# One FFT and mixture-of-experts kernel: inputs laid out in the order of its first step, the multiplier table loaded whole, and one order of steps for all eight batches

## The chip, the cores and the metric

The kernel runs on one core of one Trainium2 chip. The time is the device time of one execution in microseconds (us). Three runs of the kernel before took 1506.66, 1509.06 and 1509.7 us; the median is 1509.06 us. Work that numpy does on the host before the launch is in no time.

The core's engines are TensorE (PE in the profile, with its weight loads as PEld), VectorE (DVE), ScalarE (ACT), GpSimd (POOL) and SyncE (SP). Sixteen DMA engines move data between the chip's memory and the on-chip buffers; transfers are issued by SP, ACT and POOL, each in the order of its own queue.

## What is computed

The input x is 8 batches of 2496 rows of 256 values. Each column of each batch is filtered in the frequency domain, and the result goes through a mixture of 8 experts with a capacity of 2496 rows each:

```python
X = np.fft.rfft(x, axis=1)                      # 8 x 2496 x 256 -> 8 x 1249 x 256
Y = X * (filt_r + 1j * filt_i)[None]
y = np.fft.irfft(Y, n=2496, axis=1).reshape(19968, 256)
logits = y @ w_gate                             # 8 logits a row
# rows go to experts in the order of falling logits, at most 2496 to each expert
out[mask_e] = np.maximum(y[mask_e] @ w1[e], 0) @ w2[e]
```

## The kernel before

The program has three parts, one after the other on TensorE. Until about 404 us the batches go through the transform (class `Fft`); until 479.5 us the last step of the inverse transform runs together with the search for the experts' thresholds; from 496 us on the eight experts run. The change is in the first part and in what is loaded for it.

**The steps of one batch.** 2496 is 39 times 64. For a batch b:

- `load_x` brings x into the tile `xt`, laid out as 117 partitions (three column groups of 39 rows) by 64 by 86. `cp_x` copies `xt` into `xr`, with the 64 values of one column side by side, in two halves (24 and 19 of 43 column pairs), because the first step wants them that way. For batch 0 the copies are split over DVE and ACT; later DVE does three copies a batch and POOL one.
- `s1` (11 pieces t) multiplies each column pair of `xr` by the table `cS1` (43 matmuls) and copies the result from PSUM into `Y1`, four copies a piece, on ACT or DVE.
- `s2` (10 pieces: 5 groups g by 2 halves dh of the columns) multiplies `Y1` by the table `cW` (40 matmuls). DVE multiplies the result with the filter tile `F` into `P` and `Q`, and POOL forms the sum and the difference in place. Only two PSUM buffers hold results of `s2`, so the third piece waits until DVE's `Q` of the first has been read.
- `tr` turns the products (40 matmuls) and splits them into `yh` (ACT) and `yl` (DVE); with each second one go 8 small matmuls with the gate's weights. `trv` turns those (5 matmuls).
- `inv1` (10 pieces) does the first inverse step (60 matmuls with the tables `cEh`, `cEl`), copies to `zt` and writes it to memory as `zd`. `inv2` reads `zd` back, does the second inverse step and writes `xs`.

**What is made at the start.** `consts` loads a small table and builds `cW` from it with 20 instructions on ACT and 20 on DVE. `consts2` loads the two filters as they come, and `filt` turns them with 44 transposes on TensorE, and copies them into `F` on ACT and DVE. These turns are made to stand behind the last `s1` matmul of batch 0.

**What sets the order.** `run` gives every step a slot, ten slots a batch (`o = 10*b`), and sorts. A scheduling layer then orders each engine's instructions by those priorities. In steady state the `s1` of batch b+1 is spread over batch b's slots, `tr` follows `s2` by 3 slots and `inv1` by 5. The first three batches have rules of their own: `s1` of batch 1 stands in the last slot of batch 0, `s1` of batch 2 in the late slots of batch 1, and batch 0's `tr` and `inv1` come early:

```python
at(9.06 + t*0.08 if b == 1 else 12.4 + t*7.4/11 if b == 2 else o - 10 + t*10/11, 2, s.s1, b, t)
...
early = lambda q: 2 + 0.8*q if q < 6 else 9.1 + 0.16*(q - 6)
at(o + q + 3 if b else early(q), 3, s.tr, b, q)
```

In the trace the lines are: 193 `load_x`, 206 `cp_x`, 223 the `s1` matmuls, 231 its copies, 238 the `s2` matmuls, 244 to 247 the filter products, 257, 266 and 285 the turns, 293 `inv1`, 178 and 184 the filter's turns and copies, 130 and 131 the building of `cW`.

Of the kernel before, what the change touches and what calls it, by code (L numbers as in the profile page):

```python
# [45 lines left out]
def constants():  # L46
# [56 lines left out]

class Fft:


# [60 lines left out]
    def filt_after(s, *a):  # L167
        with s.tc.issue_after(s.mm0):
            s.filt(*a)

    def filt(s, c0, dh, ri):

        nc = s.nc
        c1 = min(c0 + 4, 11)
# [4 lines left out]
        n = 3 * (c1 - c0) if c1 < 11 else 8
        a = p[:, 0:1]  # L180
        for h in range(2):
            src = bass.AP(tensor=a.tensor, offset=a.offset + 39 * h, ap=[list(a.ap[0]), [-1 if h else 1, K1], [39, n]])
            dst = s.F[:, dh, :, 64*ri+32*h+3*c0:64*ri+32*h+3*c0+n]
            (nc.vector.tensor_copy if h else nc.scalar.copy)(dst, src)

    def load_x(s, b, j):
# [25 lines left out]
    def s1(s, b, t):  # L212
# [11 lines left out]
        if b == 0:  # L224
            s.mm0 = s.lastmm
# [940 lines left out]
```

## Time and profile before

| | us |
|---|---|
| median of three runs | 1509.06 |
| the profiled execution | 1511.66 |
| its span, first to last instruction | 1509.9 |
| first `s1` matmul | 28.6 |
| first `s2` matmul of batch 0 | 43.5 |
| first `s2` matmul of batches 1 to 7 | 97.6, 137.1, 178.4, 213.4, 253.3, 288.8, 337.8 |
| last `s2` matmul of batch 7 | 383.2 |
| last matmul before the experts' | 496 |

The profiled execution is one of its own, 2.6 us above the median; 1.8 us of it lie outside its span. The page of the profile gives the busy time of each engine over the whole span and in 40 slices of 37.7 us, with the clock that TensorE was granted. The more useful view here is a table of busy times by stretches that begin and end with a batch's first `s2` matmul. An engine's busy time on TensorE includes waiting inside its pipeline, so the pace of matmuls that follow each other without a wait says more than the share.

### The profile page before, as it was taken

The numbers are of one execution on the slowest core, as the hardware profiler recorded it, in microseconds if no ns is written. First come the engines' busy times: TensorE is split into PE (matmuls) and PEld (weight loads), VectorE is DVE, ScalarE is ACT, GpSimd is POOL, SyncE is SP. The second block draws the span as 40 slices with busy tenths as digits, with TensorE's granted clock in tenths as the row PEclk, the third lists the DMA queues.
The fourth block names the chain that finished last, engine by engine and source line by source line (L and its number), as shares of the span: only waits on it lengthen the run. The fifth ranks groups of instructions, "written<-read, shape, count | busy, mean of one in ns | idle before, by whom it ended". The sixth has DMA issues, their size and how long they took to land.

```text
span 1509.9 us, 26484 instructions
## 1 busy us (share of the span) xinstructions
PE 1409.8 (93%) x9922; PEld 1210.6 (80%) x9922; DVE 1016.8 (67%) x2686; ACT 712.4 (47%) x1687; POOL 563.4 (37%) x565
## 2 busy tenths in 40 slices
PE   2889999999897899999999999999999999999998
PEld 2778888967653788889888988888888888888887
DVE  3867877856656677966876886887887774643332
ACT  4346666643456434532643553543643553532332
POOL 0335444523300352553354354424353443333312
PEclk9989999999999899999999999999999999999999
DMA  9988784378798211110221221211211231111100
GB/s 147 192 151 151 142 158 115 83 202 251 199 342 329 81 41 70 60 50 26 88 62 34 81 66 38 88 39 50 84 53 45 93 102 48 37 53 41 44 25 27
DMA packets 114865, 150.52 MB, mean 100 GB/s; under 512 B 69403, under 2 KB 92529, under 8 KB 112433
## 3 DMA queue, kind: packets, MB, share of 16 engines
q1 hardware_dynamic: 69458, 45.68, 15.9%
q0 software_dynamic: 17840, 60.34, 12.2%
q10 hardware_dynamic: 27439, 42.82, 9.1%
q8 instruction: 78, 1.28, 0.4%
q14 instruction: 50, 0.41, 0.1%
HBM read 85.13 MB, written 63.70 MB: 99 GB/s over the span
## 4 chain that ended last, share of the span: by engine, by line
PE 42%; DVE 9%; issue 6%; ACT 2%; POOL 1%; POOLq 0%; DVEq 0%; ACTq 0%
PE pz L881 18%; PE py L935 13%; PE py L932 5%; PE py L933 3%; PE ptr L859 2%; PE rt L587 1%; DVE hl L895 1%; POOL out L949 1%; DVE w0l L839 1%; ACT lg L747 1%; DVE hl L898 1%; DVE Gm L579 1%; DVE tmp L666 1%; DVE w L839 1%; DVE OH L778 0%
## 5 line engine op out<-in xcount | busy, mean ns | idle before, releaser
L949 POOL DMA_INDIRECT out<-y,oid x160 | 173.0, 1081 | 436.6 <-ACT y L948 187.1
L935 PE MATMUL py<-w,hl 128*128 128x256 f32 x2408 | 318.0, 287 | 1.4 <-DVE loc L785 0.4
L935 PEld LDWEIGHTS py<-w,hl 128*128 128x128 f32 x2408 | 302.3, 191 | 6.0 <-DVE hl L898 0.8
L887 ACT ACTIVATE hl<-pz 128x512 fp32r<-128x512 f32 (+1 forms) x320 | 187.1, 588 | 219.5 <-PE pz L881 201.9
L881 PE MATMUL pz<-xo,w0h 128*128 128x512 f32 (+1 forms) x640 | 263.9, 412 | 6.9 <-DVE hl L895 3.4
L881 PE MATMUL pz<-xo,w0l 128*128 128x512 f32 (+1 forms) x640 | 250.0, 391 | 0.0
L881 PE MATMUL pz<-z,w0h 128*128 128x512 f32 (+1 forms) x640 | 248.7, 389 | 0.8 <-DVE z L863 0.8
L845 POOL DMA_INDIRECT xg<-xs,xid x160 | 174.9, 1093 | 158.9 <-issue 70.2
L895 DVE SCALAR_TENSOR_TENSOR hl<-pz,hl 128x512 fp32r<-128x512 f32 x227 | 155.3, 687 | 70.3 <-ACT hl L887 69.1
L932 PE MATMUL py<-w,hl 128*128 128x512 f32 x456 | 163.9, 400 | 0.2 <-ACT hl L887 0.2
L881 PEld LDWEIGHTS pz<-xo,w0h 128*128 128x128 f32 x640 | 122.5, 191 | 28.3 <-DVE hl L895 4.4
L881 PEld LDWEIGHTS pz<-xo,w0l 128*128 128x128 f32 x640 | 121.1, 189 | 24.1
L881 PEld LDWEIGHTS pz<-z,w0h 128*128 128x128 f32 x640 | 122.1, 191 | 17.4 <-DVE z L863 1.6
L933 PE MATMUL py<-w,hl 128*128 128x256 f32 x456 | 127.8, 280 | 0.2 <-DVE hl L895 0.2
L223 PE MATMUL p<-cS,xr 117*128 117x120 f32 x688 | 93.9, 287 | 36.0 <-DVE xr L206 31.4
L231 ACT COPY Y<-p 64x240 f32<-64x240 f32 (+1 forms) x288 | 110.2, 383 | 30.8 <-PE p L223 19.5
L948 ACT COPY y<-py 128x256 f32<-128x256 f32 x95 | 35.3, 372 | 183.4 <-PE py L935 146.3
L223 PEld LDWEIGHTS p<-cS,xr 117*128 117x128 f32 x688 | 88.0, 203 | 38.8 <-DVE xr L206 31.8
L246 POOL TENSOR_TENSOR P<-P 128x256 f32<-128x256 f32 x80 | 59.8, 748 | 152.6 <-DVE P L244 152.3
L238 PE MATMUL p<-cW,Y 128*128 128x128 f32 x640 | 94.3, 289 | 14.6 <-DVE Q L245 13.1
L579 DVE TENSOR_TENSOR Gm<-M,thr 117x1232 bf16<-117x1232 f32 (+2 forms) x80 | 106.5, 1342 | 0.2
L238 PEld LDWEIGHTS p<-cW,Y 128*128 128x128 f32 x640 | 84.1, 201 | 23.2 <-DVE Q L245 12.4
(235 smaller groups left out, 2482.6 us busy)
## 6 DMA issues: line engine op xcount, KB each, us to landing
zd<-zt ACTq DMA_DIRECT2D x80, 256.0 KB
xt<-x SPq DMA_DIRECT2D x24, 838.5 KB
z<-zd SPq DMA_DIRECT2D x18, 600.0 KB
xs<-xo ACTq DMA_DIRECT2D x18, 600.0 KB
xt<-zd SPq DMA_DIRECT2D x8, 600.0 KB
xs<-xt ACTq DMA_DIRECT2D x8, 600.0 KB
xs<-Y ACTq DMA_DIRECT2D x6, 600.0 KB
xg<-xs,xid POOLq DMA_INDIRECT x160, 2.8
```

The source lines that it names most:

```text
L223: s.lastmm = nc.tensor.matmul(p[:, q-q0, :120], xv[:, q-24*h], s.cS1, start=True, stop=True).ins
L231: (nc.vector.tensor_copy if t in ((5,) if b > 1 else (1, 3, 5, 7, 9)) else nc.scalar.copy)(dst, src)
L238: nc.tensor.matmul(p[:, k], s.Y1[b][:, 4*g+k, dh*128:dh*128+128], s.cW[:, 4*g+k], start=True, stop=True)
L579: nc.vector.tensor_tensor(Gm[:, s0:s1, :m], s.M[:, s0:s1].unsqueeze(2).to_broadcast([117, s1 - s0, m]), thr[:117].unsqueeze(1).to_broadcas ...
L845: s.lastg = s.nc.gpsimd.indirect_dma_start(out=xg[:n], out_offset=None, in_=s.xs, in_offset=bass.IndirectOffsetOnAxis(ap=ids[0][:n, t:t+1] ...
L881: nc.tensor.matmul(p[:, :n], w[:, sl], x[:, k, :n], start=m == 0, stop=m == 5)
L887: s.lasta = nc.scalar.activation(h[:, :n], p[:, :n], AF.Relu).ins
L895: nc.vector.scalar_tensor_tensor(l[:, :n], p[:, :n], 0.0, h[:, :n].bitcast(F32), op0=OP.max, op1=OP.subtract)
L932: nc.tensor.matmul(pp, hs[g][f][:, hi], w2[:, :, 256*f:256*f+256], start=f == 0, stop=False, skip_group_check=True)
L933: nc.tensor.matmul(pp[:, f % 2], hs[g][f][:, lo], w2h[:, 256*f:256*f+256], start=False, stop=f > 5, skip_group_check=True)
L935: nc.tensor.matmul(p[:a.stop-a.start], hs[g][f][:, a], b[:, 256*f:256*f+256], start=m == 0, stop=m == 8 * len(terms) - 1, skip_group_check ...
L949: st = nc.gpsimd.indirect_dma_start(out=out_rows, out_offset=bass.IndirectOffsetOnAxis(ap=ids[1][:w, 4*g+t:4*g+t+1], axis=0), in_=y[:w], i ...
```

## The change

Three inputs are now prepared on the host. `xl` holds x in the order that `s1` reads, so that `load_x` fills `xr` itself with long rows (4 to 12 KB a partition), and `cp_x`, `cp_after` and the tile `xt` are gone. `fl` holds the filter as `F` wants it; `filt`, its transposes and its copies are gone. `cW` is the finished table (1.31 MB instead of 148 KB), loaded by SP.

The start is rewritten: four pieces of x of batch 0, then `cW`, the gate's weights, two fifths of `F`, a part of batch 1's x, the rest of `F`, the rest of that x. Nine matmuls on a zeroed tile (128 by 512, 16 bit) stand ahead of the first `s1`. The tables `cEh` and `cEl` are still loaded by POOL, after the last piece of `F`.

The rules for the first batches are gone: all batches have `s1` at `o - 10 + t*10/11`, `tr` at `o + q + 3`, `inv1` at `o + q + 5`, and x of batch b+2 is asked for at `o + 0.1`. The copies from PSUM of `s1` of batch 1 go mostly to ACT, as those of the later batches do. The double-buffered x tile is now all that the first part keeps of x, so more of the memory beside it is free earlier.

```diff
+def laid(x, fr, fi):
+    v = x.reshape(B, N1, N2, D)
+    xl = np.empty((B, 3, N1, 43, 2, N2), np.float32)
...
+    F = np.stack([f[at] for f in (fr, fi)], 1).reshape(5, 4, 2, J, 2, 128)
...
-        nc.scalar.dma_start(s.zt0[1][:, :296], i['cW'])
...
-        for k in range(K1):
-            nc.scalar.activation(s.cW[:, k], ab[:, :128], AF.Copy, scale=cs[:, k:k+1])
-            nc.vector.scalar_tensor_tensor(s.cW[:, k], ab[:, 128:], cs[:, K1+k:K1+k+1], s.cW[:, k], op0=OP.mult, op1=OP.add)
+        for _ in range(9):
+            nc.tensor.matmul(p, r[:, :128], r, start=True, stop=True)
...
-    def filt(s, c0, dh, ri):
...
-    def cp_x(s, b, h):
...
+    def load_x(s, b, q0, q1):
+        if q0 == 0:
+            s.xr[b] = s.xp.tile([128, 43, 2 * N2], F32, name="xr", bufs=2)[:117]
+        s.lastld = s.nc.sync.dma_start(s.xr[b][:, q0:q1].rearrange("p q n -> p (q n)"), s.i['xl'][b, :, 128*q0:128*q1]).ins
...
-                at(9.06 + t*0.08 if b == 1 else 12.4 + t*7.4/11 if b == 2 else o - 10 + t*10/11, 2, s.s1, b, t)
...
+                at(o - 10 + t*10/11, 2, s.s1, b, t)
...
-                at(o + q + 3 if b else early(q), 3, s.tr, b, q)
+                at(o + q + 3, 3, s.tr, b, q)
```

**Three places in the order of instructions.** On SP, the first transfers of the program. Before, three pieces of x (39 partitions each, `xt_134`), then the filters, then batch 1's x (`xt_168`):

```order
L121 DMA cS1_84<-cS1 117x120
L193 DMA xt_134<-x 39x64x86 x3
L145 DMA Y1_150<-filt_r 117x10x256
L145 DMA Y1_150<-filt_r 1x10x256
L146 DMA P_88<-filt_r 78x256
L147 DMA P_88<-filt_r 1x256
L145 DMA Y1_150<-filt_i 117x10x256
```

Now:

```order
L136 DMA cS1_84<-cS1 117x120
L184 DMA xr_103<-xl 117x1024 x2
L184 DMA xr_103<-xl 117x1536
L184 DMA xr_103<-xl 117x1920
L150 DMA cW_87<-cW 128x2560
L164 DMA gate_112<-moe_w_gate 128x8 x2
L154 DMA F_86<-fl 128x2048
L184 DMA xr_123<-xl 117x3072
L154 DMA F_86<-fl 128x3072
L184 DMA xr_123<-xl 117x2432
```

The table `cW` and the first two fifths of the filter stand between batch 0's x and batch 1's.

On TensorE, behind the last `s1` matmuls of batch 0. Before, the filter's turns (`pa<-fid,Y1_150`) with the first two pieces of `s2` (line 238) among them:

```order
L223 MATMUL p1_269<-cS1_84,xr1_143 128x120 x3
L178 MATMUL pa_277<-fid_148,Y1_150 128x118 x4
L178 MATMUL pa_284<-fid_148,Y1_150 128x118 x4
L178 MATMUL pa_291<-fid_148,Y1_150 128x118 x2
L178 MATMUL pa_291<-fid_148,P_88 128x79
L178 MATMUL pa_297<-fid_148,Y1_150 128x118 x4
L238 MATMUL p2_359<-cW_87,Y1_178 128x128 x4
L238 MATMUL p2_370<-cW_87,Y1_178 128x128 x4
```

Now, a little later in batch 0, from the fourth piece of `s2` (line 207) on; line 226 is `tr`, 235 the gate's matmuls, 194 the `s1` of batch 1 (`xr_123`):

```order
L207 MATMUL p2_305<-cW_87,Y1_133 128x128 x4
...
L235 MATMUL pv_354<-P_270,gate_112 32x128 x4
L194 MATMUL p1_244<-cS1_84,xr_123 128x120 x4
L194 MATMUL p1_256<-cS1_84,xr_123 128x120 x4
L207 MATMUL p2_334<-cW_87,Y1_133 128x128 x4
L254 MATMUL pv_365<-fid_111,vs_363 128x128
L226 MATMUL pa_389<-fid_111,P_290 128x128
L207 MATMUL p2_378<-cW_87,Y1_133 128x128 x4
L194 MATMUL p1_276<-cS1_84,xr_123 128x120 x4
```

The `s1` of batch 1 has moved from behind batch 0 in between its pieces of `s2`.

On DVE, a stretch of batch 3. Before, a copy of x (`xr1_1700<-xt_858`) stands between a product `P` and the product `Q` (`Q_1612`) of the same piece, whose reading frees the PSUM buffer for TensorE:

```order
L244 TENSOR_TENSOR P_1611<-p2_1606,F_85 128x512
L206 COPY xr1_1700<-xt_858 117x19x64
L288 TENSOR_TENSOR Vl_147<-pv_1564,Vh_146 128x4x8
L307 COPY zt_1588<-pa_1589 128x512
L279 TENSOR_TENSOR yl_1585<-pa_1579,yh_1584 128x512
L279 TENSOR_TENSOR yl_1626<-pa_1620,yh_1625 128x512
L244 TENSOR_TENSOR P_1668<-p2_1663,F_85 128x512
L245 TENSOR_TENSOR Q_1612<-p2_1606,F_85 128x512
```

Now, at about the same place:

```order
L213 TENSOR_TENSOR P_1657<-p2_1652,F_86 128x512
L214 TENSOR_TENSOR Q_1658<-p2_1652,F_86 128x512
L257 TENSOR_TENSOR Vl_110<-pv_1601,Vh_109 128x4x8
L276 COPY zt_1634<-pa_1635 128x512
L248 TENSOR_TENSOR yl_1631<-pa_1625,yh_1630 128x512
L248 TENSOR_TENSOR yl_1669<-pa_1663,yh_1668 128x512
L213 TENSOR_TENSOR P_1711<-p2_1706,F_86 128x512
L214 TENSOR_TENSOR Q_1712<-p2_1706,F_86 128x512
```

The copy is gone, and `Q` stands right behind its `P`. From the last part of batch 7 on, the instructions on every engine stand in the same order in both programs, but for four of the transfers of `zd` on SP, which now stand earlier.

## Rows read from the trace of the kernel before

**Rows 1.** The page: the span, TensorE's busy time, and its busy share and granted clock in 40 equal slices (tenths).

```profile
span 1509.9 us, 26484 instructions
...
PE 1409.8 (93%) x9922; PEld 1210.6 (80%) x9922; DVE 1016.8 (67%) x2686; ACT 712.4 (47%) x1687; POOL 563.4 (37%) x565
...
PE   2889999999897899999999999999999999999998
...
PEclk9989999999999899999999999999999999999999
```

**Rows 2.** Busy times by stretches: from batch to batch (each begins with a batch's first `s2` matmul), and the stretch after 404 us. Columns: from and to, length, busy us and instructions of PE, PEld, DVE, ACT, POOL, the granted clock, the DMA engines' share, GB/s.

```profile
43.50:97.60 54.10, 43.72 (x383) 38.73 (x381) 39.48 (x75) 22.30 (x60) 17.30 (x21) 0.93 1.02 201
97.60:137.10 39.50, 34.90 (x303) 31.53 (x303) 33.15 (x42) 21.95 (x58) 23.36 (x21) 0.93 0.69 115
137.10:178.40 41.30, 37.85 (x359) 36.18 (x356) 31.74 (x46) 26.61 (x71) 18.66 (x22) 0.96 0.79 146
178.40:213.40 35.00, 31.88 (x326) 29.86 (x325) 29.77 (x46) 21.61 (x57) 17.62 (x20) 1.00 0.88 151
213.40:253.30 39.90, 36.78 (x353) 34.38 (x351) 29.49 (x49) 26.24 (x69) 18.22 (x21) 0.96 0.74 159
253.30:288.80 35.50, 33.99 (x346) 32.17 (x346) 29.40 (x48) 23.54 (x62) 19.27 (x22) 1.00 0.27 67
288.80:337.80 49.00, 45.73 (x355) 36.61 (x353) 28.81 (x53) 27.09 (x68) 14.61 (x21) 0.97 0.63 173
337.80:383.20 45.40, 42.86 (x375) 35.20 (x374) 30.40 (x62) 15.90 (x38) 16.60 (x34) 0.96 0.84 236
...
404.00:479.50 75.50, 71.49 (x323) 38.51 (x322) 49.38 (x186) 46.90 (x106) 6.89 (x6) 1.00 0.93 332
```

**Rows 3.** The timeline of the head, on SP, ACT, DVE and PE. Columns: start, length, engine and line, what it does, how many, and in brackets the idle time before it and what ended it. SPq and ACTq rows are the issuing of transfers.

```profile
1.23 12.42 SPq L193 DMA_DIRECT2D xt<-x  x3
1.44 0.37 ACTq L124 DMA_DIRECT2D P<-cW  x1
4.08 5.94 ACT L130 ACTIVATE cW<-P 128x128 f32<-128x128 f32 x20 [0.75 <-DMA P<-cW]
...
27.18 4.15 DVE L206 COPY xr<-xt 117x512 f32<-117x512 f32 x4 [16.78 <-DMA xt<-x]
28.63 1.64 PE L223 MATMUL p<-cS,xr 117*128 117x120 f32 x6 [28.63 <-DVE xr L206]
...
41.37 0.97 PE L178 MATMUL pa<-fid,Y 118*128 118x118 f32 x8
43.52 1.96 PE L238 MATMUL p<-cW,Y 128*128 128x128 f32 x16
...
47.31 0.68 DVE L244 TENSOR_TENSOR P<-p,F 128x512 f32<-128x512 f32 x1
```

**Rows 4.** Busy times (columns as in Rows 2) of four short stretches: x of batch 0 alone on the DMA engines, the two halves of its `s1` (in the first the filters move), and a stretch in which `zd` is read and `xs` written in long rows.

```profile
10.00:20.00 10.00, 0.00 (x0) 0.00 (x0) 0.40 (x2) 0.02 (x1) 0.00 (x0) 1.00 1.08 142
28.60:35.00 6.40, 6.37 (x30) 6.37 (x31) 4.37 (x6) 6.28 (x8) 0.00 (x0) 1.00 0.92 190
35.00:41.50 6.50, 6.50 (x60) 6.50 (x60) 5.47 (x14) 5.38 (x15) 0.31 (x2) 1.00 1.01 140
430.00:440.00 10.00, 9.96 (x48) 5.11 (x47) 6.00 (x19) 6.08 (x13) 0.00 (x0) 1.00 0.95 385
```

**Rows 5.** The timeline of TensorE where matmuls follow each other without a wait; from one row's start to the next row's is the pace. The trace holds two instructions for each matmul of lines 223, 238 and 266, one for the others.

```profile
83.39 0.27 PE L285 MATMUL pv<-fid,vs 128*128 128x128 f32 x1
83.49 1.05 PE L223 MATMUL p<-cS,xr 117*128 117x120 f32 x8
84.38 0.60 PE L257 MATMUL pa<-fid,P 128*128 128x128 f32 x4
84.82 1.05 PE L223 MATMUL p<-cS,xr 117*128 117x120 f32 x8
85.80 0.65 PE L266 MATMUL pv<-P,gate 128*32 128x128 f32 x16
86.37 0.39 PE L293 MATMUL pa<-yh,cEh 128*128 128x256 f32 x1
...
111.40 0.28 PE L293 MATMUL pa<-yh,cEl 128*128 128x256 f32 x1
111.52 1.05 PE L238 MATMUL p<-cW,Y 128*128 128x128 f32 x8
112.41 1.05 PE L223 MATMUL p<-cS,xr 117*128 117x120 f32 x8
```

**Rows 6.** First the sum over the five stretches from 97.6 to 288.8 us and the next one of the busy time of line 206 alone, the copies of x. Then what TensorE waited for, in total, times, longest, from 97.6 to 288.8 us and from 43.5 to 97.6 us. Then two copies of x of the same size on DVE, and a product on POOL that ran during the first.

```profile
sum 240.20, DVE 40.27 ACT 0.00 POOL 20.43; mean DVE 6.71 ACT 0.00 POOL 3.40
...
PE p L238 <- DVE Q L245: 8.7, 6, 3.0
...
PE p L238 <- DVE Q L245: 3.7, 5, 1.5
...
202.21 3.81 DVE L206 COPY xr<-xt 117x1216 f32<-117x1216 f32 x1
238.36 1.62 DVE L206 COPY xr<-xt 117x1216 f32<-117x1216 f32 x1 [2.07 <-PE p L223]
204.58 1.98 POOL L246 TENSOR_TENSOR P<-P 128x256 f32<-128x256 f32 x1
```

More of the change, by code (lines that the diff above doesn't have):

```diff
@@ L101, in constants @@
                 cPw=pw.reshape(128, 77).astype(f), cInt=ic.astype(np.uint32).view(np.int32), cTri=tri.astype(f))
+def laid(x, fr, fi):
+    v = x.reshape(B, N1, N2, D)
+    xl = np.empty((B, 3, N1, 43, 2, N2), np.float32)
+    for j in range(3):
+        for c in range(2):
+            d = 85 * j + 43 * c
+            xl[:, j, :, :, c] = v[..., d:d+43].transpose(0, 1, 3, 2)
+    j, k = np.arange(J)[None], np.arange(K1)[:, None]
+    at = np.where(j < 32, k + 39 * j, 39 * (j - 31) - k)
+    F = np.stack([f[at] for f in (fr, fi)], 1).reshape(5, 4, 2, J, 2, 128)
+    return dict(xl=xl.reshape(B, 117, 43 * 2 * N2), fl=np.ascontiguousarray(F.transpose(5, 0, 4, 1, 2, 3)).reshape(128, -1))
 class Fft:
@@ L222, in s1 @@
         for q in range(q0, q1):
-            s.lastmm = nc.tensor.matmul(p[:, q-q0, :120], xv[:, q-24*h], s.cS1, start=True, stop=True).ins
-        if b == 0:
-            s.mm0 = s.lastmm
+            nc.tensor.matmul(p[:, q-q0, :120], s.xr[b][:, q], s.cS1, start=True, stop=True)
         for cp in range(2):
@@ L230, in s1 @@
                 dst = bass.AP(tensor=a.tensor, offset=a.offset, ap=[list(a.ap[0]), [a.ap[1][0], K1], [85, 3], [1, q1-q0]])
-                (nc.vector.tensor_copy if t in ((5,) if b > 1 else (1, 3, 5, 7, 9)) else nc.scalar.copy)(dst, src)
+                (nc.vector.tensor_copy if t in ((5,) if b else (1, 3, 5, 7, 9)) else nc.scalar.copy)(dst, src)
     def s2(s, b, g, dh):
@@ L306, in inv1 @@
         last = b == B - 1
-        x = (nc.scalar.copy if last else s.cps[q % 2])(zt, p)
-        if (b, q) == (0, 2):
-            s.zc = x.ins
+        (nc.scalar.copy if last else s.cps[q % 2])(zt, p)
         if q % 2:
@@ L422, in run @@
         at(-12, 0, s.consts)
[L423 to L430 removed]
+        for q in ((0, 8), (8, 16), (16, 28), (28, 43)):
+            at(-12, 0, s.load_x, 0, *q)
+        at(-12, 1, s.load_w, 0, K1)
+        at(-12, 1, s.consts2)
+        at(-12, 2, s.load_f, 0, 2)
+        at(-12, 2, s.load_x, 1, 0, 24)
+        at(-12, 2, s.load_f, 2, 5)
+        at(-12, 3, s.consts3)
+        at(-12, 3, s.load_x, 1, 24, 43)
         for b in range(B):
             at(10*(b // 2) + 16, 9, s.no_time, b)
[L433 to L436 removed]
         for b in range(B):
@@ L439, in run @@
             for t in range(11):
[L441 to L445 removed]
+                at(o - 10 + t*10/11, 2, s.s1, b, t)
             if b + 2 < B:
[L447 to L448 removed]
+                for q in ((0, 24), (24, 43)):
+                    at(o + 0.1, 8, s.load_x, b + 2, *q)
             for g in range(5):
@@ L451, in run @@
                     at(o + 2*g + dh, 1, s.s2, b, g, dh)
-                at(o + 2*g + (4.5 if b else 3.5), 3.5, s.trv, b, g)
+                at(o + 2*g + 4.5, 3.5, s.trv, b, g)
             for q in range(10):
-                early = lambda q: 2 + 0.8*q if q < 6 else 9.1 + 0.16*(q - 6)
-                at(o + q + 3 if b else early(q), 3, s.tr, b, q)
+                at(o + q + 3, 3, s.tr, b, q)
                 if b < B - 1 or q < 2:
-                    at(o + q + I1 if b else early(q + 2) + 0.01, 4, s.inv1, b, q)
+                    at(o + q + I1, 4, s.inv1, b, q)
         at(10*B - 20, 0, s.early)
@@ L1158 @@
     arrays = {n: np.ascontiguousarray(inputs[n]) for n in _INS}
+    arrays.update(laid(*(np.asarray(inputs[n], np.float32) for n in ('x', 'filt_r', 'filt_i'))))
     arrays.update(constants())
```

98 lines of the change are left out of this document (21 added, 77 removed).

## The prediction

> **What bounds the kernel now.** I read the page first, then the stretches by batch, then the head, and last the pace of single matmuls. TensorE is busy for 93% of the span, and the slices in which it is not are the first four: 2, 8, 8 and 9 tenths, with the granted clock down in the third [rows 1]. The experts, from 496 us on, keep it at 9 tenths and their instructions stand in the same order in both programs, so the change can only act on the first 404 us.
>
> There are two losses there. The first is the head: x of batch 0 is asked for at 1.23 us and DVE's first copy of it starts at 27.18, after 16.78 us of idle time that a DMA ended; TensorE's first matmul is at 28.63, its first `s2` at 43.52 and the first filter product at 47.31 [rows 3]. The second is that a batch takes longer than its matmuls. A busy share doesn't show that, the pace does. From row to row in a stretch without waits [rows 5] one `s1` matmul takes 0.89 us / 4 = 0.222 us, one of `s2` the same, a turn 0.44 / 4 = 0.11, a gate matmul 0.57 / 8 = 0.071, one of `inv1` 0.12, one of `trv` 0.10. By the counts in the order of instructions, batches 1 to 5 before hold 423 matmuls of `s1` and `s2`, 184 turns, 184 gate, 258 `inv1`, 22 `trv`: 93.9 + 20.2 + 13.1 + 31.0 + 2.2 = 160.4 us. They take 288.8 - 97.6 = 191.2 us [rows 2], so 30.8 us, 6.2 a batch, are waits and low clock. Batch 0 takes 54.1 us [rows 2] for about 37 us of matmuls.
>
> **The change, part by part.** I work out when batch 7's `s2` begins, at 337.8 us before [rows 2]. What stands behind that is the same work in the same order.
>
> *The head.* A transfer of 148 KB was issued at 1.44 us and used at 4.08, 2.6 us later [rows 3]. The first piece of x is 479 KB, issued at about 1.6 us; at 385 GB/s, the rate of long rows [rows 4], it is 1.2 us of transfer, and without the 0.4 us that the 148 KB took `s1` starts at about 5. Before, `s1` took from 28.6 to 41.5 and `s2` began at 43.5, 14.9 us after `s1`'s start; that gives 19.8 us. But in the first 6.4 us of it TensorE issued 30 instructions and in the next 6.5 us 60 [rows 4]: twice the pace, the ratio of 1.2 to 2.4 GHz, though the column shows 1.00 for both. If the nine matmuls on zeros bring the higher level earlier, up to 3.2 us are saved: 16.6. I take 18.5 for the start of `s2`, nearer to the measured row, since ACT's copies, which took part in that stretch, stay. The filter's turns go from this path as well (41.37 to 47.31, [rows 3]), which the 14.9 us already contain in part.
>
> The Trainium skill, "TensorE: Matmul & The Clock Gate", section "What's actually happening", says that the low clock is the default and that activity releases it. By that rule the nine matmuls would do it before x is there, and the sum would be 1.9 us lower; row and rule agree on the cold start, and whether matmuls on zeros count as activity no run here shows yet.
>
> *What must have come by then.* The small tables, x of batch 0, `cW` and two fifths of `F` are 0.11 + 2.58 + 1.31 + 1.05 = 5.05 MB. The first byte comes at about 3.4 us: 1.23 and the 2.6 us of that small transfer, less the 0.4 us that 148 KB take. At 385 GB/s [rows 4] all have come by 16.5 us, inside 18.5. The other bound is 190 GB/s, what the filters' 1 KB rows moved at in the first half of `s1` [rows 4]: 30.0 us, 11.5 us too late. The new rows are 4 to 20 KB, so I take the first. The rest of `F`, 1.57 MB behind 1.44 MB of x, lands by 24.3 us and is needed by the fifth piece of `s2`, about 24 (DVE needs 1.2 us a piece); the two tables `cE` behind it, 2.62 MB, by about 34, needed at about 41, since the order puts all of batch 1's `s1` ahead of the first `inv1`.
>
> The Trainium skill, "DMA: Bandwidth & Descriptors", section "Why a DMA increments its semaphore by 16 and not by 1", speaks against the rate: a transfer uses the largest number of engines up to 16 that divides its outer sizes. By that rule 117 partitions would use 13 engines and the 120 of [rows 4] 15, so x would take 7.7 us instead of 6.7; the sum would be at most 1 us higher.
>
> *Batch 0.* Up to batch 1's first `s2` the new order holds 91 matmuls of `s1` and `s2`, 20 turns, 16 gate, 12 `inv1`, 2 `trv`: 20.2 + 2.2 + 1.1 + 1.4 + 0.2 = 25.1 us. What is left to wait for is DVE's `Q` at the first pieces, where TensorE has nothing else: 3.7 us before [rows 6]. I take 5, since the pipeline now fills with less other work: 30.1 us instead of 54.1. The bounds are 25 and 35.
>
> *Batches 1 to 5.* The new order holds 411 matmuls of `s1` and `s2`, 212 turns, 216 gate, 324 `inv1`, 26 `trv`: 91.2 + 23.3 + 15.3 + 38.9 + 2.6 = 171.3 us, 11 more than before, because work that batch 0 finished at its own end now lies here. Of the waits, the largest is `s2` for DVE's `Q`, 8.7 us [rows 6], and in DVE's queue a copy of x stood before that `Q`. The copies took 40.3 us of DVE and 20.4 us of POOL in these batches [rows 6]; they were slow because they met POOL (3.81 us against 1.62 for the same copy, and a product of POOL took 1.98 during the slow one, [rows 6]). Without them DVE is busy for about 153.6 - 40.3 = 113.3 us of 191.2, ACT for 120 [rows 2], POOL for less: TensorE is left as the bound. The best batch before, 253.3 to 288.8, holds 83 matmuls of `s1` and `s2`, 40 turns, 40 gate, 54 `inv1` and 5 `trv`, 32.7 us, and took 35.5 with the copies in it [rows 2], 2.8 us more. I take 2.5 a batch: 183.8 us. Bounds: 0 and the old 6.2 a batch, 171.3 and 202.3.
>
> *Batch 6.* No copy of x stood in it, and the second inverse step of two batches lies in it in both programs. By the counts the new one holds 4 matmuls of `s1` and `s2` more and 8 turns, 8 gate, 18 `inv1` and 1 `trv` less: +0.9 - 0.9 - 0.6 - 2.2 - 0.1 = -2.9 us. I keep its waits: 49.0 [rows 2] - 2.9 = 46.1 us.
>
> *Behind it.* Batch 7 (45.4 us) and the stretch from 404 to 479.5, where TensorE is busy for 71.5 of 75.5 us [rows 2], move as they are. Four reads of `zd` now stand earlier on SP, ahead of x of batches 6 and 7; each waits for a batch that `inv1` has finished by then, and what is queued behind it is x that is needed ten slots later. I cost it at nothing; if that cover were gone, `s1` of batch 6 would wait. A gain of up to 3 us in the later stretch is possible, as its DMA share is 0.93 [rows 2].
>
> *Work that is hidden before and after:* building `cW` on ACT (5.94 us, [rows 3]) ran while x was awaited.
>
> Sum: 18.5 + 30.1 + 183.8 + 46.1 = 278.5 us against 337.8. The span falls by 59.3 us, from 1509.9 to 1450.6, the execution from 1511.66 to 1452.4. The median of the runs is 2.6 us below that execution, so against it the forecast is 1509.06 - 59.3, about 1450.
>
> **The rivals.**
>
> *The waits stay.* If a batch loses 6.2 us without the copies too (`yl` waits for ACT's `yh`, `Q` for POOL), batches 1 to 5 take 18.5 us more: 1468. For it: 8.7 us of `s2`'s waits in 30.8 are few [rows 6], and the rest is spread. Against it: the batch from 253.3 on, which lost 2.8 with its copies.
>
> *The head stays slow.* Long rows at 190 GB/s put `s2` at 30: 1461.
>
> *Tighter than I think.* No waits in batches 1 to 5 (-12.5) and the clock up early (-1.9): 1436, and a few us less if the later stretch gains.
>
> *Slower than before.* Short waits in place of long work could leave TensorE at 1.2 GHz. In the stretches by batch the clock column is 0.93 to 1.00 [rows 2], by length times twice the missing share about 26 us at the low level in all. Each us at that level costs half a us of matmuls, so the whole gain is gone if another 118 of the 320 us to batch 7's end ran at 1.2 GHz, and beyond that the kernel is slower: 150 us would give 1450 + 75 = 1525. Against it: the two batches with a clock of 1.00 [rows 2] are those that lost least, and waits are what the change removes. The page on the clock gate in the Trainium skill (section "HAM oscillation — how this bites in real kernels") describes such a fall from waits between bursts of matmuls; no row here shows it for waits as short as `s2`'s.
>
> *It doesn't do what it says:* the first filter product could wait for all of `F`. The order lets it wait for the first transfer of `F` alone, so this has no chance of its own.
>
> **How the numbers follow.** My forecast, within 9 us of 1450, has 0.55; the waits stay 0.17; the slow head 0.09; tighter 0.16; slower than before 0.015; and 0.015 that losses I don't see eat the gain to within 0.2%, about what a measurement of this kernel can tell from no change. The range for 8 in 10 takes in most of the first rivals and both ends of the batches' term: 1435 to 1470. Faster by over 0.2% is then 0.97.
>
> **What would show it.** Right: first `s1` at about 5 us, first `s2` at 17 to 20; batches 1 to 5 at 34 to 38 us each, with DVE busy for under 25 us in each and POOL's products at 0.74 us; batch 7's `s2` beginning at about 279; from there to the first expert as long as before. Wrong: an idle TensorE at the start that a DMA ends, batches that still take 39 to 41 us, a clock column below 0.93, or `s1` of batch 6 waiting for x.

## The result and the profile after

The changed kernel took 1457.89 to 1464.54 us in four runs, median 1460.07; the kernel before took 1506.66 to 1512.24 beside it, median 1509.38. The ratio is 0.9678 (95% interval 0.9657 to 0.9699), a gain of 49 us where 59 were forecast. The profiled execution took 1464.54 us, the longest of the four. First its page: span, busy time by engine, TensorE in 40 slices, and its clock.

```profile
span 1462.7 us, 26256 instructions
...
PE 1398.0 (96%) x9887; PEld 1201.0 (82%) x9887; DVE 956.2 (65%) x2614; ACT 704.3 (48%) x1669; POOL 534.7 (37%) x558
...
PE   7889999998997999999999999999999999999998
...
PEclk9999999999998999999999999999999999999999
```

The nearly empty first slice of before [rows 1] is gone: 7 tenths instead of 2. Where the rest went shows in the stretches by batch (columns as in [rows 2]); the last one runs from the last `s2` to the filler matmuls ahead of the experts.

```profile
20.60:58.40 37.80, 31.02 (x249) 28.01 (x250) 15.60 (x28) 19.93 (x54) 14.46 (x22) 0.91 0.92 273
58.40:94.60 36.20, 35.81 (x364) 33.99 (x363) 25.64 (x45) 24.27 (x63) 14.43 (x20) 1.00 0.55 164
94.60:135.70 41.10, 37.41 (x367) 35.22 (x366) 26.89 (x49) 26.44 (x70) 14.51 (x20) 0.92 0.40 114
135.70:173.80 38.10, 36.13 (x353) 34.47 (x352) 25.36 (x46) 24.32 (x64) 15.44 (x22) 0.96 0.55 163
173.80:209.90 36.10, 36.10 (x369) 34.54 (x368) 25.29 (x46) 26.28 (x69) 15.19 (x21) 1.00 0.61 175
209.90:247.10 37.20, 35.95 (x375) 33.85 (x374) 25.40 (x47) 26.08 (x69) 14.56 (x20) 1.00 0.50 150
247.10:287.60 40.50, 40.50 (x318) 33.18 (x317) 25.92 (x47) 24.77 (x63) 13.23 (x19) 1.00 0.76 212
...
333.10:437.00 103.90, 91.78 (x496) 54.32 (x494) 64.63 (x213) 57.14 (x129) 10.93 (x10) 0.93 0.88 292
```

Set against the forecast, in us; the last column is a version of the experiments below, with three more edits:

| stretch | before | forecast | after | three edits more |
|---|---|---|---|---|
| up to the first `s2` | 43.5 | 18.5 | 20.6 | 17.6 |
| batch 0 | 54.1 | 30.1 | 37.8 | 32.1 |
| batches 1 to 5 | 191.2 | 183.8 | 188.7 | 178.1 |
| batch 6 | 49.0 | 46.1 | 40.5 | 40.5 |
| batch 7 | 45.4 | 45.4 | 45.5 | 46.9 |
| last `s2` to the filler matmuls | 96.3 | 96.3 | 103.9 | 99.9 |
| to the first expert matmul | 16.4 | 16.4 | 14.7 | 15.3 |
| experts | 1014.0 | 1014.0 | 1011.0 | (slower chip) |

So the head and batch 0 gave 39.2 us, batch 6 another 8.5, batches 1 to 5 only 2.5, and the late stretch took 7.6 back. Six of the eight rows are off by 2 us or more, in both directions. Part of that is one execution's chance: a second profile of the same kernel (run 9 below) has 19.7, 40.2, 185.8, 40.5, 44.6 and 104.0 us in the first six rows, so 2 to 3 us between two profiles mean little. Three places in the trace say why the rows differ from the forecast.

**The head and batch 0.** TensorE, then one row of DVE, then TensorE again (start, length, what, and in brackets the idle time and what ended it):

```profile
1.23 4.02 PE L147 MATMUL p<-P 128*128 128x512 f16 x9 [1.23 <-DVE P L143]
5.79 3.94 PE L194 MATMUL p<-cS,xr 117*128 117x120 f32 x32 [0.54 <-DMA xr<-xl]
11.20 2.91 PE L194 MATMUL p<-cS,xr 117*128 117x120 f32 x24 [1.47 <-DMA xr<-xl]
15.52 3.58 PE L194 MATMUL p<-cS,xr 117*128 117x120 f32 x30 [1.41 <-DMA xr<-xl]
20.61 2.05 PE L207 MATMUL p<-cW,Y 128*128 128x128 f32 x16 [1.52 <-ACT Y L200]
...
31.44 0.69 DVE L213 TENSOR_TENSOR P<-p,F 128x512 f32<-128x512 f32 x1 [2.45 <-DMA F<-fl]
...
47.76 0.97 PE L194 MATMUL p<-cS,xr 117*128 117x120 f32 x3 [3.25 <-DMA xr<-xl]
```

`s1` starts at 5.8 (the forecast was about 5), but x's later pieces are waited for twice; the filter's second part is late for DVE; and at 47.76 `s1` of batch 2 waits 3.25 us for its x. SP shows why that is crowded: the rest of x of batch 1 and x of batches 2 and 3 stand in one row there.

```profile
11.09 34.18 SPq L184 DMA_DIRECT2D xr<-xl  x5
```

Busy times of five stretches (last columns: clock, DMA share, GB/s):

```profile
5.80:20.60 14.80, 10.42 (x86) 9.86 (x86) 8.13 (x20) 9.08 (x24) 0.00 (x0) 1.00 1.01 310
20.00:28.00 8.00, 6.78 (x64) 5.85 (x65) 5.49 (x10) 1.78 (x5) 4.97 (x7) 1.00 0.82 326
28.00:52.00 24.00, 19.17 (x145) 18.31 (x145) 7.27 (x14) 15.90 (x42) 6.63 (x12) 0.89 0.98 266
46.60:53.40 6.80, 5.64 (x38) 5.26 (x38) 0.00 (x0) 0.00 (x0) 0.00 (x0) 0.50 0.92 245
97.80:104.60 6.80, 5.26 (x36) 4.84 (x37) 4.47 (x8) 1.19 (x3) 2.87 (x4) 0.50 0.19 53
```

While `s1` of batch 0 runs, the DMA engines are busy throughout and move 310 GB/s, where the forecast had 385. From 20 to 28 us they are busy for 0.82 of the time, at 326 GB/s: 2.61 MB move there, the first 1.44 MB of batch 1's x and, behind it on SP, the rest of the filter. Before, 120 rows moved at 385 and a share of 0.95 [rows 4]. From 28 to 52 us the rest of batch 1's x, x of batch 2, asked for as soon as its buffer is free, and the tables `cE` share the engines. The last two rows are the stretches at half clock that go with the wait at 47.76 and with one in batch 2: 6.8 us each, of which TensorE is busy for 5.6 and 5.3, so they cost 2.8 and 2.6 us of matmuls.

**A wait that takes the old one's place.** In batches 1 to 5, no wait of `s2` for `Q` is left among the long ones [rows 6]. Instead, in the table of waits up to 335 us (total, times, longest):

```profile
PE p L194 <- DMA xr<-xl: 6.7, 4, 3.3
PE pv L235 <- DVE zt L276: 4.0, 2, 3.7
...
PE pa L262 <- DVE zt L276: 2.9, 2, 2.0
...
DVE zt L276 <- DMA zd<-zt: 12.3, 4, 5.3
```

The longest of them in the timeline:

```profile
85.23 1.30 ACTq L279 DMA_DIRECT2D zd<-zt  x2
85.45 0.73 SPq L184 DMA_DIRECT2D xr<-xl  x2
...
98.60 0.69 DVE L276 COPY zt<-pa 128x512 f32<-128x512 f32 x1 [5.34 <-DMA zd<-zt]
...
99.34 1.08 PE L235 MATMUL pv<-P,gate 128*32 128x128 f32 x16 [3.69 <-DVE zt L276]
```

Two writes of `zt` are issued from 85.23 on; at 85.45 SP asks for all 2.58 MB of x of batch 4 (x of batches 2 and 3 stands in the row of five above). `zt` has two buffers, used in turns, so the copy at 98.6 needs the one that those writes read: 13 us after their issue. Behind it on DVE stands what TensorE waits for.

**The late stretch.** Its rows on ACT, with a wait that before did not have:

```profile
398.01 0.40 ACTq L382 DMA_DIRECT2D xs<-Y  x1
...
402.83 1.84 ACT L379 COPY xo<-pv 120x512 f32<-120x512 f32 x4 [4.85 <-DMA xs<-Y]
```

The instruction order tells what each program's first copy into the new tile `xo` (pool `zo`) must wait for, by the names of semaphores (those with DMA in them stand for transfers); first after, then before:

```
L379 COPY xo<-pv 120x512 [waits DMAHW4_49,DMAHW1_49,DMAHW7_49,DMAHW0_49,PE_49]
L412 COPY xo<-pv 120x512 [waits PE_49,Pool_49]
```

`Y1` has two buffers, used in turns. Before, the raw filters took the first turn (`fl` is a tile of that name); without it each later `Y1` lies in the other buffer, and in the late stretch, where four stores leave from the last `Y1`, that is the one that `zo` is laid over. So a transfer deleted at the start made a new wait 400 us later.

### The profile page after: what moved, and what is told of

It is laid out like the page before. It is cut to its first block, busy times and chain, and to the rows that moved or that the text cites. A ratio compares the mean times of both kernels' runs of the same rounds, so it can differ in the third digit from the quotient of the medians.

```text
span 1462.7 us, 26256 instructions
## 1 busy us (share of the span) xinstructions
PE 1398.0 (96%) x9887; PEld 1201.0 (82%) x9887; DVE 956.2 (65%) x2614; ACT 704.3 (48%) x1669; POOL 534.7 (37%) x558
## 3 DMA queue, kind: packets, MB, share of 16 engines
q1 hardware_dynamic: 9422, 47.03, 10.5%
## 4 chain that ended last, share of the span: by engine, by line
PE 44%; DVE 9%; issue 6%; ACT 3%; POOL 1%; POOLq 0%; DVEq 0%; ACTq 0%
PE pz L839 19%; PE py L893 13%; PE py L890 5%; PE py L891 3%; PE ptr L817 2%; PE rt L545 1%; DVE hl L853 1%; POOL out L907 1%; DVE w0l L797 1%; ACT lg L705 1%; DVE hl L856 1%; DVE Gm L537 1%; ACT hl L845 1%; DVE M L622 1%; DVE w L797 1%
## 5 line engine op out<-in xcount | busy, mean ns | idle before, releaser
L893 PEld LDWEIGHTS py<-w,hl 128*128 128x128 f32 x2408 | 300.3, 190 | 6.1 <-DVE hl L856 0.8
L200 ACT COPY Y<-p 64x240 f32<-64x240 f32 (+1 forms) x304 | 116.2, 382 | 29.6 <-PE p L194 17.2
L215 POOL TENSOR_TENSOR P<-P 128x256 f32<-128x256 f32 x80 | 58.5, 731 | 191.2 <-DVE P L213 190.9
L890 PEld LDWEIGHTS py<-w,hl 128*128 128x128 f32 x456 | 85.7, 188 | 19.9 <-ACT hl L845 0.5
L207 PE MATMUL p<-cW,Y 128*128 128x128 f32 x640 | 88.1, 277 | 2.5 <-ACT Y L200 1.5
```

The source lines that it names most:

```text
L200: (nc.vector.tensor_copy if t in ((5,) if b else (1, 3, 5, 7, 9)) else nc.scalar.copy)(dst, src)
L207: nc.tensor.matmul(p[:, k], s.Y1[b][:, 4*g+k, dh*128:dh*128+128], s.cW[:, 4*g+k], start=True, stop=True)
L890: nc.tensor.matmul(pp, hs[g][f][:, hi], w2[:, :, 256*f:256*f+256], start=f == 0, stop=False, skip_group_check=True)
L893: nc.tensor.matmul(p[:a.stop-a.start], hs[g][f][:, a], b[:, 256*f:256*f+256], start=m == 0, stop=m == 8 * len(terms) - 1, skip_group_check ...
```

## The experiments

All are edits of the changed kernel, but the eleventh, of the kernel before. The first four ran on a chip where the kernel before took 1509.5 us, the others on two chips where it took 1527; the difference lies in the experts, 1011.0 us in the profile above and 1027.9 in the ninth run's. Across chips I compare ratios, or stretches ahead of the experts.

**1. Two more buffers for `zt`.**

```diff
-            s.zt = s.wp.tile([128, 4, D], F32, name="zt", bufs=ZB)
+            s.zt = (s.xp if b < B - 2 and (5*b + q // 2) % 4 > 1 else s.wp).tile([128, 4, D], F32, name="zt", bufs=ZB)
```

> Two more buffers for the tile zt in batches 0 to 5, nothing else. Theory (zt's writes to zd queue behind x on the DMA engines, so that zt is not free, TensorE waits and the clock falls): the waits on zt go (12.3 us of DVE in 4 waits, 6.9 of TensorE), batch 2 (94.6 to 135.7) falls from 41.1 to about 36.5 and batch 3 from 38.1 to about 36, batch 0 stays at 37.8; in all 6 to 9 us less, about 1452. Rival (these waits only stand in place of others, such as that for DVE's products, and the clock falls anyway): within 2 us of 1460.

Measured: 1450.84 us (1446.44 to 1451.5), ratio 0.9602 (0.9558 to 0.9646). The busy times of batches 2 and 3, and the wait of DVE for `zd`:

```profile
95.00:130.00 35.00, 35.00 (x368) 33.10 (x366) 25.86 (x48) 26.22 (x70) 14.53 (x20) 1.00 0.48 132
130.00:164.40 34.40, 34.40 (x354) 32.81 (x353) 25.50 (x46) 24.29 (x64) 15.47 (x22) 1.00 0.52 151
```

```profile
DVE zt L276 <- DMA zd<-zt: 0.7, 1, 0.7
```

In these two batches TensorE is busy throughout and the clock is 1.00; batches 1 to 5 take 178.2 us instead of 188.7 (185.8 in run 9), and batch 0 stays (38.1). The theory holds and the rival is out: nothing took the place of these waits.

**2. x on 128 rows.**

```diff
-    return dict(xl=xl.reshape(B, 117, 43 * 2 * N2), ...
+    return dict(xl=np.pad(xl.reshape(B, 117, 43 * 2 * N2), ((0, 0), (0, 11), (0, 0))), ...
```

(and the tile's 128 rows are loaded, 117 of them multiplied.)

> x laid out on 128 rows, the last 11 of them zeros, so 9% more bytes. Theory (a transfer of 117 rows is spread over 13 of the 16 DMA engines, which the DMA share of 0.82 at 326 GB/s between 20 and 28 us speaks for): where x moves alone the share is over 0.95 and the rate about 390 GB/s, the first s2 starts 1 to 2 us sooner than 20.6, and the whole is 1 to 4 us less, 1456 to 1459. Rival (the rate has another bound, such as the size of the rows): rate unchanged, the pieces of x land 9% later, the first s2 at 21 to 22, the whole 0 to 2 us more.

Measured: 1450.25 us (1446.48 to 1453.44), ratio 0.9611 (0.9564 to 0.9658). TensorE's start in the timeline, then busy times of two short stretches of x's transfers, of batch 0, and of batches 1 to 5:

```profile
5.29 10.29 PE L194 MATMUL p<-cS,xr 117*128 117x120 f32 x86
17.08 2.05 PE L207 MATMUL p<-cW,Y 128*128 128x128 f32 x16 [1.50 <-ACT Y L200]
```

```profile
8.00:12.00 4.00, 4.00 (x38) 4.00 (x38) 3.66 (x10) 3.55 (x10) 0.00 (x0) 1.00 1.02 429
18.00:22.00 4.00, 3.40 (x34) 2.83 (x33) 3.17 (x5) 0.00 (x0) 2.67 (x4) 1.00 1.00 419
17.10:49.20 32.10, 28.49 (x248) 25.70 (x249) 15.48 (x28) 18.72 (x50) 14.29 (x22) 1.00 0.91 367
49.20:229.50 180.30, 175.94 (x1797) 167.23 (x1796) 127.19 (x228) 127.48 (x332) 74.37 (x103) 1.00 0.52 157
```

9% more bytes arrive sooner: behind the head the share goes from 0.82 to 1.00 and the rate from 326 to 419 GB/s, `s1` runs in one piece, the first `s2` is 3.5 us sooner and batch 0 takes 32.1 instead of 37.8. Batches 1 to 5 take 180.3 instead of 188.7, nearly as little as in run 1, though `zt` has its two buffers: DVE's wait for `zd` falls from 12.3 to 7.4 us and the clock stays at 1.00. The expectation's price was too low (9.8 us, not 1 to 4), since it looked at the head alone, and its mechanism is only a part: in the head the share was full before and after, at 310 and 429 GB/s, so there more than idle engines was at work. What that was, no run shows.

**3. No matmuls on zeros.**

```diff
-        for _ in range(9):
+        for _ in range(0):
```

> Without the nine matmuls on zeros at the start. If they raised the clock ahead of x: the granted clock is low for the first 3.4 us of s1, the first s2 moves from 20.6 to 21 to 23, since x's pieces are waited for in that stretch anyway (1.5, 1.4 and 1.5 us), and the whole is 0 to 2.5 us more. If matmuls on zeros do not count: no change in the clock's record and none in the time.

Measured: 1468.19 us (1458.66 to 1472.08), ratio 0.9718 (0.9658 to 0.9778). The first `s1` in the timeline, and the busy times of its two halves:

```profile
5.73 9.24 PE L194 MATMUL p<-cS,xr 117*128 117x120 f32 x56 [5.73 <-DMA xr<-xl]
```

```profile
5.70:11.50 5.80, 5.77 (x27) 5.80 (x28) 1.62 (x4) 1.83 (x5) 0.00 (x0) 1.00 1.04 284
11.50:20.30 8.80, 7.05 (x61) 6.71 (x60) 6.51 (x16) 7.26 (x20) 0.00 (x0) 1.00 0.99 334
```

27 instructions of `s1` (the trace has two for each matmul) now take 5.8 us, where the changed kernel did 32 in 3.9: the zeros do raise the clock (the column shows 1.00 for both; the pace tells). The low pace lasted 5.8 us, not the 3.4 expected. Yet the first `s2` starts at 20.3, no later, since x sets it. What the whole costs is unclear: the profiled execution reaches the filler matmuls 2.4 us later (439.4 against 437.0), the median is 8 us higher, and the intervals overlap.

**4. x asked for later, in quarters.** ACT writes one element of each piece behind a `yh`, and the transfer must wait for that.

```diff
-                for q in ((0, 24), (24, 43)):
-                    at(o + 0.1, 8, s.load_x, b + 2, *q)
+                for c, q in zip((1.1, 3.1, 5.1, 7.1) if b else (4.1, 5.6, 7.1, 8.6), ((0, 12), (12, 24), (24, 34), (34, 43))):
+                    at(o + c, 8, s.load_x, b + 2, *q)
...
+            with s.tc.issue_after(s.lyh): s.nc.scalar.copy(s.xr[b][64:65, q0, :1], s.warm[64:65, :1])
```

> x of batches 2 to 7 in four pieces, each asked for behind one of ACT's yh (the tiny copy that stands for that is 0.2 us, four a batch), spread over the batch, instead of two pieces as soon as the buffer is free. Theory (x of batch 2 crowds out cE, F and itself between 28 and 52 us, and in later batches the writes of zd): batch 0 falls from 37.8 to 31 to 34, the wait of s1 for x (3.3) and for cEl go, the waits for zt go or fall to under 3 us in all, batches 1 to 5 from 188.7 to about 182; in all 8 to 13 us less, about 1450. Rival (the order itself makes the waits): batch 0 stays within 1.5 us and the whole within 3.

Measured: 1452.12 us (1445.83 to 1453.95), ratio 0.9612 (0.9563 to 0.966). Batch 0 takes 32.7, batches 1 to 5 180.5, and no wait for `zt` is left; batch 7 gives 4.6 us back (50.1, with a wait of 2.3 us for a read of `zd`). So a third remedy is worth about the same, 8 us, and since it changes only when x is asked for, the losses in batch 0 and in `zt` have one source: those transfers, too early and too slow.

**5. and 10. The place of `Y1`.** One element is written into a `Y1` at the start, so that the turns fall as before; the first copy into `zo` then waits for `PE_49,Pool_49` alone.

```diff
+        y = s.wp.tile([128, K1, D], F32, name="Y1", tag="Y1", bufs=2)
...
+        nc.gpsimd.memset(y[:1, 0, :1], 0.0)
```

> One element written at the start into a buffer of the tile Y1, so that the two buffers of Y1 are taken in turns as in the kernel before and the stores of the late second inverse step leave from the other one (in the changed kernel the first new tile xo lies where that buffer was, and ACT's copy waits 4.9 us for its last store). Theory (this place in memory is what cost the stretch from the last s2 to the filler matmuls its 103.9 us instead of 96.3): the wait goes, the low clock behind it too, the stretch takes 96 to 99, the whole 5 to 8 us less, 1452 to 1455. Rival (the stretch is bound by its transfers, at a DMA share of 0.95, and the wait moves elsewhere): within 2 us of 1460.

> The changed kernel itself, to stand beside the next three on one chip. Its ratio to the kernel before lies in 0.966 to 0.970, and the first s2 at 20 to 21 us, the last at 330 to 335.

> The place of Y1 once more (one element written at the start into one of its buffers), beside the changed kernel on the same chip. Theory (the late stretch loses what its profile showed, 103.9 against 98.4 us): 4 to 6 us less than the changed kernel. Rival (that was one profile's luck, and a wait at another place takes it back before the end): within 1.5 us of it.

Measured: the fifth run 1475.52 us on the second chip, ratio 0.9669 (0.9625 to 0.9713), with a late stretch of 98.4 us. On the third chip the changed kernel (9) took 1480.26 (0.9695, 0.9665 to 0.9725) and this edit (10) 1475.69 (0.9658, 0.9624 to 0.9693), 4.6 less, as expected, though the intervals overlap. The late stretch of the ninth and ACT's wait in it, then the same of the tenth:

```profile
330.80:434.80 104.00, 90.22 (x494) 53.88 (x493) 64.29 (x213) 56.59 (x127) 10.77 (x10) 0.95 0.87 283
```

```profile
ACT xo L379 <- DMA xs<-Y: 6.3, 1, 6.3
```

```profile
333.70:431.90 98.20, 90.37 (x495) 54.10 (x493) 63.02 (x213) 57.21 (x129) 11.37 (x10) 0.95 0.91 305
```

```profile
ACT xo L379 <- DMA xs<-Y: 2.0, 2, 1.4
```

ACT's wait is shown: its longest wait for `xs<-Y` is 0.6 to 2.8 us in the four runs with this edit (5, 6, 10, 12) and 4.8 to 7.1 in the nine profiles in which the raw filters no longer take the first turn and nothing else does. What it costs is less clear. The stretch itself takes 98.4 and 98.2 with the edit alone against 103.9 and 104.0, but 102.0 and 99.9 in runs 6 and 12, which have it too, and 100.0 and 99.8 in runs 1 and 8, which do not. For the whole time the gain is likely, not certain.

The ninth run itself missed one expectation by a little: its first `s2` starts at 19.7, not at 20 to 21. Its ratio and its last `s2`, at 330.8, came as expected.

**6. and 12. The three edits together** (1, 2 and 5).

> Three edits at once: x on 128 rows, two more buffers for zt, and the place of Y1. If the three remedy different losses (x's rate in the head and in batch 0; zt in batches 1 to 3; the store in the late stretch), the sum holds: 9.8 for x, about 8 for zt of which the faster x has taken some, 5 to 8 for Y1, so 1436 to 1442. If they all remedy the same loss (crowded DMA engines), it is no better than the best of them, 1447 to 1450.

> The three edits at once (x on 128 rows, two more buffers for zt, the place of Y1) beside the changed kernel on the same chip. If each remedies a loss of its own: 17 to 22 us less than the changed kernel, ratio to the kernel before 0.953 to 0.957. If they share one: 9 to 12 less.

Measured: ratio 0.9546 (0.9504 to 0.9587) on the second chip, 1458.03 us; on the third 1459.37 us, ratio 0.9557 (0.9528 to 0.9586), 20.9 us below the changed kernel beside it and clear of its interval. The twelfth, batch 0 and batches 1 to 5:

```profile
17.60:49.70 32.10, 28.47 (x249) 25.70 (x250) 15.51 (x28) 18.72 (x51) 14.31 (x22) 1.00 0.89 361
49.70:227.80 178.10, 177.31 (x1819) 168.31 (x1818) 128.67 (x230) 128.13 (x333) 74.31 (x103) 1.00 0.51 150
```

This version beats both kernels, and in batches 1 to 5 TensorE is now idle for 0.8 us in 178. The whole time is what the sum expects, more than the rival of one shared loss. But the stretches don't show three separate losses: x on 128 rows alone (run 2) already takes batches 1 to 5 to 180.3 us, so there it and the two buffers remedy for the most part the same waits. From the start to the filler matmuls the changed kernel takes 437.0 us (434.8 in run 9), run 2 420.0, and the three edits 417.3 and 415.1.

**7. The old slots.** `s1` of batches 1 and 2, the turns, `trv` and first inverse step of batch 0, and the engines for batch 1's `Y1` as before.

```diff
-                at(o - 10 + t*10/11, 2, s.s1, b, t)
+                at(9.06 + t*0.08 if b == 1 else 12.4 + t*7.4/11 if b == 2 else o - 10 + t*10/11, 2, s.s1, b, t)
...
-                at(o + q + 3, 3, s.tr, b, q)
+                at(o + q + 3 if b else early(q), 3, s.tr, b, q)
```

> The layouts of the changed kernel with the slots of the kernel before for s1 of batches 1 and 2, for the turns, trv and first inverse step of batch 0, and its choice of engine for batch 1's Y. Theory (one step order for all is part of the gain, since batch 0's wait for its own inverse step is filled with s1 of batch 1): batch 0 and 1 together 6 to 12 us longer, the whole 1466 to 1472. Rival (with x there early, the order does not matter, or the old one hides the transfers of cE better): 1457 to 1462.

Measured: ratio 0.9649 (0.9602 to 0.9696), the changed kernel's own within the intervals. Batches 0 and 1 take 39.6 and 38.8 (4.4 us more, where 6 to 12 were expected; 1.8 more than in run 9), batch 2 34.9 (6.2 less), and the last `s2` ends at 330.5 instead of 333.1. My theory falls: with x laid out, one order for all batches is worth nothing that these runs can tell.

**8. Copies of x put back,** into a tile that nobody reads, for batches 2 to 7.

```diff
+        for c, eng in enumerate((vec, s.nc.gpsimd.tensor_copy if h else vec)):
+            eng(d[:, :, c], x[:, :, 43*c+24*h:43*c+24*h+w].rearrange("p n q -> p q n"))
```

> The copies of x put back for batches 2 to 7 on DVE and POOL, with the old shapes and in the old slots, into a tile that nobody reads, so that they cost engine time alone and s1 does not wait for them. Theory (a batch lost to them, since the filter's products Q stand behind them on DVE and POOL is slowed): batches 1 to 5 go from 188.7 to 198 to 207, the wait of s2 for Q comes back (8.7 before), the whole 1469 to 1478. Rival (DVE is busy for 26 of 37 us a batch and takes them in its idle time): batches 1 to 5 within 3 us, the whole within 3 of 1460.

Measured: 1523.59 us, ratio 0.9989 (0.9963 to 1.0015): the whole gain is gone, far more than expected. Part of that is not the copies' work: in batch 0 (48.0 us) DVE stood 15.6 us in front of a copy whose x had not landed. Batch 1 (60.1 us) holds the copies of two batches, 16.2 us of DVE, with a wait of 2.0 for x, and batch 2 (30.4) holds none. In batches 3 to 5, where the wait for x is 5.9 us in all, the busy times are these, and behind them the sum of the copies' own:

```profile
159.90:200.20 40.30, 36.40 (x354) 34.56 (x353) 30.53 (x49) 24.30 (x64) 18.44 (x23) 0.96 0.41 122
200.20:243.70 43.50, 36.83 (x353) 34.90 (x351) 32.10 (x46) 24.64 (x65) 19.95 (x20) 0.92 0.40 125
243.70:287.60 43.90, 37.22 (x353) 35.36 (x352) 33.78 (x49) 25.59 (x67) 21.48 (x22) 0.88 0.39 119
```

```profile
sum 127.70, DVE 23.08 POOL 12.39; mean DVE 7.69 POOL 4.13
```

127.7 us against 111.4: 5.4 a batch, with DVE at 32.1 of 42.6. Even if all 5.9 us of waiting for x were passed on, 10.4 of the 16.3 us would be the copies' own, so the rival (DVE takes them in its idle time) is out; how the rest divides stays open. The theory named the wrong wait, though: in these batches TensorE waited 13.4 us for DVE's `Vl`, which stands behind a copy as well, and 2.0 for `Q`.

**11. The filter alone, in the kernel before.** `fl` and `F` as in the change, the transposes gone; x, its copies and the order stay.

> The kernel before with one part of the change alone: the filter laid out by numpy as the table F, its transposes gone; x, its copies, the building of cW and the order stay. Theory (x's own way through DMA and copies sets the head, and the transposes filled a wait): s1 starts at 26 to 28.6 us, the first s2 at 40 to 42.5 instead of 43.5, the first product 3 to 4 us sooner, the batches after batch 0 as before; in all 4 to 8 us less than before, ratio 0.995 to 0.997. Rival (the transposes and the short rows of the filters set the head as much as x does): the first s2 at 35 or sooner, the whole 12 to 20 less.

Measured: 1526.85 us beside 1526.95, ratio 0.9997 (0.9979 to 1.0015). The first `s2` starts at 42.5, the first product 3.6 us sooner than before [rows 3]; here that product, and ACT's wait in the late stretch:

```profile
43.69 0.69 DVE L226 TENSOR_TENSOR P<-p,F 128x512 f32<-128x512 f32 x1 [1.68 <-PE p L220]
```

```profile
ACT xo L394 <- DMA xs<-Y: 8.0, 2, 6.3
```

The last `s2` ends 3.0 us sooner, and the late stretch takes 106.2 instead of 96.3, with the wait for `xs<-Y` that this kernel, too, has for want of the tile `fl`. So this part gains nothing alone, where 4 to 8 us were expected. The order of the steps (run 7) brings nothing that can be told either, and the zeros (run 3) at most the 8 us between the medians, so what is left for most of the gain is x's layout, and with it the copies. That is by exclusion: no run has x's layout alone in the kernel before, and the finished table `cW` was not tried apart.

## Why the prediction was right, and where it was off

*The head* (18.5, measured 20.6). Start and clock were right: x at 5.8, `s1` at full pace after the zeros. Off was "I take the first" for the rate: 385 GB/s was read from 120 rows, and with x on 117 the head had 310; with 128 rows the term is 17.1, within the forecast's bounds. (The new rows are 4 to 12 KB long, not "4 to 20".) By the rule of the Trainium skill, "DMA: Bandwidth & Descriptors", section "Why a DMA increments its semaphore by 16 and not by 1", 117 rows use 13 engines, and the trace agrees from 20 to 28 us: a share of 0.82 is 13 of 16 (though behind x the rest of the filter, on 128 rows, moves there too). The prediction weighed that rule and priced it at 1 us at most; the second run shows that 128 rows are worth 3.5 us in the head, 5.7 more in batch 0 and 8.4 in batches 1 to 5 (of one profile each), and in the head not by the number of engines alone.

The Trainium skill, "TensorE: Matmul & The Clock Gate", section "What's actually happening", says that activity releases the low clock; matmuls on zeros count as such, by the third run. The first `s2` gained nothing by it, as x was late.

*Batch 0* (30.1, measured 37.8; bounds 25 to 35). The failed step is "`cE` ... by about 34, needed at about 41": the sum of bytes left out x of batch 2, which SP asks for as soon as `s1` of batch 0 has read its buffer. TensorE still waited for `cEl` at 57.3 us (0.9), and before that for x of batch 2: 3.25 us of wait and 2.8 by the low clock, most of the 7.7. Runs 2 and 4, with x faster or later, bring 32.1 and 32.7.

*Batches 1 to 5* (183.8, measured 188.7). Right: the copies stood in front of `Q`, and without them that wait went, and DVE's load fell to 25 to 27 us a batch (forecast: under 25). Missing: the writes of `zd` that share the DMA engines with x's transfers, and so a new wait. It cost 10.5 us (run 1 against this profile; 7.6 against run 9's), and what is then left, 178.2, is below the forecast: the allowance of 2.5 us a batch for other waits was too much.

*Batch 6* (46.1, measured 40.5). "I keep its waits" was wrong: TensorE is busy for 40.5 of 40.5 us, and before it was idle for 3.3 of 49.0 [rows 2], in which it waited for reads of `zd` (3.3 us in two waits).

*Behind it* (unchanged or 3 less, measured 7.6 more up to the filler matmuls). "Move as they are" failed on a thing that no order of steps shows: which of two buffers a tile gets. How much of the 7.6 us that made stays open (runs 5, 6, 10 and 12).

*The rivals.* "The waits stay" (1468) was nearest to what came, with other waits than the old ones. "Slower than before" through the clock did not come; the clock column fell as low as 0.91 and 0.92 only in the two batches with the longest waits, and there waits of 3.3 and 3.7 us went with 6.8 us at 1.2 GHz each. The Trainium skill, "TensorE: Matmul & The Clock Gate", section "HAM oscillation — how this bites in real kernels", describes such a fall; here it added 2.8 and 2.6 us to these two waits.

Of the signs of being wrong that the prediction named, three came: a TensorE that waits for a DMA in the head, a batch of 41.1 us, and a clock below 0.93. And 1460 lies just outside "within 9 us of 1450", to which it gave 0.55, though inside 1435 to 1470.

The losses that I missed (head 2.1, batch 0 7.7, batches 1 to 5 4.9, late stretch 7.6) are 22.3 us, those I overrated (batch 6 5.6, the rest 4.6) 10.2; the difference is the 12.1 us by which the profiled span, 1462.7, stands above the forecast one, 1450.6. The right sum owes something to errors that cancel.

## What to carry to other kernels

When copies are replaced by larger transfers, add up the bytes of all that the queue will ask for once a buffer is free, not only of what is needed next, and look at who writes through the same DMA engines with few buffers behind it. A layout made by the host costs little to pad to 128 rows, and that was worth about 10 us here, where the old order of the first steps could not be told from the new one. When a tile is deleted from a pool whose buffers go round, compare what the later users of that memory wait for.

## What the runs showed of the hardware

With x on 117 rows the DMA engines moved 310 GB/s in the head at a share of 1.01, and 326 at 0.82 from 20 to 28 us; with 128 rows it was 429 at 1.02 and 419 at 1.00. Matmuls on zeros raised TensorE's clock: 32 instructions of `s1` in 3.9 us after them, 27 in 5.8 without. Two writes issued 0.2 us ahead of 2.58 MB of x were still waited for 13 us later. And one program's experts part took 1011.0 us on one chip and 1027.9 on another, at like clock (0.982 and 0.98 over the span).
